# Transposing the probabilities of eleven pairs of heads in the DMA engines instead of TensorE

## Chip, cores and metric

One core of a Trainium2 chip. The metric is the device time of one execution in microseconds; below it is called the time. TensorE (PE, with its weight loads as PEld), VectorE (DVE), ScalarE (ACT) and GpSimd (POOL) compute, SyncE (SP) issues the DMA transfers.

## What is computed

Attention of 8 batches of 8 heads over 576 positions of 64 values, with a mask by blocks of 64 positions, then a mixer on the result: a step along the positions of rank 32, and a feed-forward step over 512 channels with 2048 hidden ones.

```
scores = scale * matmul(q, k.T);  masked where the key's block is later than the query's
attn = exp(scores - max);  attn = attn / (sum(attn) + 1e-09)
x = matmul(attn, v), heads side by side: [batch, 576, 512]
u = x + (x.T @ U @ V).T
out = u + max(u @ w_ch1, 0) @ w_ch2
```

## The kernel before

**Pairs of heads.** The 64 heads go in 32 pairs p of two heads s. The queries of a head lie in five blocks i: 64 queries in block 0, 128 in the others, and block i sees 128 i + 64 keys. `scores` multiplies queries by keys on TensorE in fp32, takes the largest score on VectorE (L1287) and the exponentials with their sums on ScalarE (L1298); they land in SBUF in `pt_r`, queries on the partitions. `normalise` inverts the sums (L1311, L1312) and scales the exponentials in place on GpSimd (L1319), twelve instructions to a pair. `transpose` turns them block by block on TensorE into PSUM (L1373), 26 to a pair, and eight copies to a pair bring them to `pw_r` in SBUF: on ScalarE (L1346), two of the eight on VectorE (L1344) from pair VP on. `apply_v` multiplies by V in fp32 (L1394): the two heads write the upper and lower 64 partitions of one bank, 16 instructions to each head. `mix` does the step along the positions (L1426 to L1480) and stores u.

**The mixer.** `ffn_chunk` does 768 of the hidden channels for chunks of 288 positions, two chunks to a batch, in three half-precision products for each fp32 one (L729, L754): 72 products in either line for each chunk. A chunk needs u of its batch, so its four pairs. `block_products` does the other 1280 channels for whole batches in seven products in place of eight (L978). It starts once all pairs are through (`end`), and has its weights split into high and low parts: `weights` casts them on ScalarE (L835) and subtracts on GpSimd (L831). The first weights go where the pool `ep` was, so they wait for what used that pool (`scored`, L811).

**The order of the work.** `Plan` takes each piece of work with an engine, an estimated duration, a rank and what it reads and writes. `issue` then plays the estimates through: an engine that is free takes the ready piece of the lowest rank. The sequence that comes out is the program of each engine, and at run time each engine follows its program in order and waits where something isn't ready. Pairs have ranks of 2000 p and some, mixer products on TensorE 1e6 and more, so these fill in where no piece of a pair is ready. Where nothing is ready in the first 130 us, a product of zeros is put in (L1560). `port` marks VectorE's pieces during which the plan starts none on GpSimd. VARIANT seeds a variation of +-2% on the estimates.

## Time and profile before

| | us |
|---|---|
| time, median of 3 runs (lowest, highest) | 1076.58 (1076.16, 1077.4) |
| time of the profiled execution | 1076.24 |
| its span, first to last instruction | 1074.4 |
| TensorE busy in the span | 1065.3 |
| VectorE, ScalarE, GpSimd busy | 850.3, 650.7, 346.3 |
[...]
| first and last product with V (L1394) | 24.6, 576.37 |
| DMA | 107.37 MB, 100 GB/s |

Busy time is the union of an engine's instructions. Products on TensorE overlap, so what one costs is read from one start to the next in the timeline, not from its duration. An engine's lines also say what ended the idle time before them.

### The profile page before, as it was taken

The numbers are of one execution on the slowest core, as the hardware profiler recorded it, in microseconds if no ns is written. First come the engines' busy times: TensorE is split into PE (matmuls) and PEld (weight loads), VectorE is DVE, ScalarE is ACT, GpSimd is POOL, SyncE is SP. The second block draws the span as 40 slices with busy tenths as digits, with TensorE's granted clock in tenths as the row PEclk, the third lists the DMA queues.
The fourth block names the chain that finished last, engine by engine and source line by source line (L and its number), as shares of the span: only waits on it lengthen the run. The fifth ranks groups of instructions, "written<-read, shape, count | busy, mean of one in ns | idle before, by whom it ended". The sixth has DMA issues, their size and how long they took to land.

```text
span 1074.4 us, 25473 instructions
## 1 busy us (share of the span) xinstructions
PE 1065.3 (99%) x9676; PEld 845.8 (79%) x9676; DVE 850.3 (79%) x1799; ACT 650.7 (61%) x1674; POOL 346.3 (32%) x624
## 2 busy tenths in 40 slices
PE   9999999999999999999999999999999999999998
PEld 7678867888787888888877777777777777777776
DVE  5879987887764665778856643999898989999998
ACT  6888777766766667577585542545454545454553
POOL 4744436556545455365376460000000000000000
PEclk9999999999999999999999999999999999999999
DMA  4453635453433241444222422040404031313111
GB/s 146 136 175 121 201 107 186 137 174 116 130 103 101 82 131 63 151 132 160 89 80 74 127 59 75 1 126 9 133 13 122 18 116 32 103 37 98 41 50 45
DMA packets 68266, 107.37 MB, mean 100 GB/s; under 512 B 6896, under 2 KB 50928, under 8 KB 68144
## 3 DMA queue, kind: packets, MB, share of 16 engines
q1 hardware_dynamic: 68144, 105.75, 31.8%
q8 instruction: 76, 1.25, 0.5%
q14 instruction: 46, 0.38, 0.1%
HBM read 76.23 MB, written 29.49 MB: 98 GB/s over the span
## 4 chain that ended last, share of the span: by engine, by line
PE 93%; ACT 3%; DVE 2%; POOL 1%; issue 1%; DMA 0%; ACTq 0%; POOLq 0%; DVEq 0%
PE bb L978 38%; PE bf L754 13%; PE bf L729 12%; PE ba L1373 8%; PE ba L1394 8%; PE bw L1262 5%; PE bq L1262 3%; ACT p L1298 2%; PE ba L1426 2%; PE ba L1452 1%; PE ba L1480 1%; PE bf L1560 1%; POOL p L1319 1%; POOL w1l L831 0%; PE bf L1120 0%
## 5 line engine op out<-in xcount | busy, mean ns | idle before, releaser
L1319 POOL TENSOR_SCALAR p<-p,rv 64x64 f32<-64x64 f32 (+4 forms) x384 | 183.5, 490 | 111.1 <-DVE rv L1312 35.3
L978 PE MATMUL bb<-ph,w2h 128*128 128x288 f16 x560 | 151.1, 286 | 0.0
L978 PE MATMUL bb<-ph,w2l 128*128 128x288 f16 x560 | 151.1, 286 | 0.0
L978 PE MATMUL bb<-ph,w1l 128*128 128x288 f16 x560 | 148.8, 286 | 0.0
L978 PE MATMUL bb<-ph,w1h 128*128 128x288 f16 x560 | 148.8, 286 | 0.0
L900 ACT CAST ph<-hb 128x576 f16<-128x576 f32 x144 | 84.3, 589 | 83.1 <-PE bb L978 82.0
L978 PEld LDWEIGHTS <-w1h 128*128 128x128 f16 x1120 | 109.3, 98 | 28.0
L978 PEld LDWEIGHTS <-w2h 128*128 128x128 f16 x1120 | 109.3, 98 | 27.9
L978 PE MATMUL bb<-pl,w2h 128*128 128x288 f16 x560 | 123.7, 286 | 0.0
L1287 DVE TENSOR_REDUCE mx<-bw 128x1 f32<-128x576 f32 (+2 forms) x192 | 76.2, 436 | 50.1 <-PE bw L1262 49.2
L978 PE MATMUL bb<-pl,w1h 128*128 128x288 f16 x560 | 114.5, 286 | 0.0
L754 PE MATMUL bf<-hh,w2h 128*128 128x288 f16 x384 | 110.3, 287 | 0.4 <-DVE hl L737 0.4
L754 PE MATMUL bf<-hh,w2l 128*128 128x288 f16 x384 | 110.0, 286 | 0.6 <-DVE w2l L543 0.6
L754 PE MATMUL bf<-hl,w2h 128*128 128x288 f16 x384 | 109.9, 286 | 0.0
L1373 PE MATMUL ba<-ident,p 128*128 128x128 f32 x668 | 102.2, 276 | 0.0
L1298 ACT ACTIVATE p<-bw,mx 128x192 f32<-128x192 f32 (+2 forms) x192 | 92.5, 489 | 13.9 <-DVE mx L1287 12.0
L1262 PE MATMUL bw<-raw 64*64 64x288 f32 (+4 forms) x896 | 97.0, 346 | 0.4 <-ACT p L1298 0.3
L902 DVE TENSOR_TENSOR pl<-hb,ph 128x576 f16<-128x576 f32 x144 | 91.2, 650 | 1.5
L729 PEld LDWEIGHTS <-w1h 128*128 128x128 f16 x768 | 74.2, 98 | 19.9 <-issue 2.3
L1262 PE MATMUL bq<-raw 64*64 64x384 f32 (+1 forms) x496 | 89.7, 470 | 0.1
L754 PEld LDWEIGHTS <-w2h 128*128 128x128 f16 x768 | 75.1, 98 | 18.5 <-ACT w2h L539 0.2
L1373 PEld LDWEIGHTS ba<-ident,p 128*128 128x128 f32 x668 | 76.8, 141 | 5.6 <-issue 1.6
(193 smaller groups left out, 2386.5 us busy)
## 6 DMA issues: line engine op xcount, KB each, us to landing
raw<-in_qk_dram SPq DMA_DIRECT2D x31, 576.0 KB, 3.9
o_d<-ot SPq DMA_DIRECT2D x72, 144.0 KB, 1.8
vr<-in_v_dram SPq DMA_DIRECT2D x32, 320.0 KB, 3.0
ur<-u_d SPq DMA_DIRECT2D x64, 144.0 KB, 2.3
wr<-o_d SPq DMA_DIRECT2D x32, 288.0 KB, 3.1
out_dram<-wr SPq DMA_DIRECT2D x31, 288.0 KB, 2.3
st<-in_w_dram SPq DMA_DIRECT2D x16, 512.0 KB, 4.2
u_d<-ut SPq DMA_DIRECT2D x28, 288.0 KB, 2.1
```

The lines of the kernel that those rows point to most:

```text
L729: nc.tensor.matmul(ps[:, :T], w()[wn][:, k, fs], m[k].ap, start=(i == 0), stop=(i == len(ops) - 1))
L754: nc.tensor.matmul(ps[:, :T], w()[wn][:, f, ms], hs[f][x].ap, start=(i == 0), stop=(i == len(ops) - 1))
L900: add("ACT", _act(n * T, True), E, lambda: nc.scalar.copy(h.ap[:, :n, :], x[0]()), [x[1]], [h])
L902: "DVE", _dve(n * T), E, lambda: nc.vector.tensor_sub(l.ap[:, :n, :], x[0](), h.ap[:, :n, :]), [x[1], h], [l],
L978: nc.tensor.matmul(bank[:, i, :T], x()[:, w(k)], p.ap[:, k, :], start=first and n == 0, stop=last and n == len(ops) - 1)
L1262: nc.tensor.matmul(o, raw[r, 64 * n : 64 * n + 64], raw[r, S + k0 : S + k1], start=True, stop=True)
L1287: lambda i=i, n=n: nc.vector.tensor_reduce(out=mx[: P if i else 64, n : n + 1], in_=view(i), op=ALU.max, axis=AX.XY if i == 4 else AX.X, n ...
L1298: return nc.scalar.activation(out.rearrange("p (j k) -> p j k", j=2) if i == 4 else out, view(i), AF.Exp, bias=mx[:rows, n : n + 1], accum ...
L1319: lambda: nc.gpsimd.tensor_scalar(out=out, in0=x, scalar1=iv, scalar2=1.0, op0=ALU.mult, op1=ALU.mult),
L1373: nc.tensor.transpose(out=to, in_=pt_r[i][h % PB[i]][:, j * P : (j + 1) * P], identity=perm.ap)
L1394: nc.tensor.matmul(bank[g][64 * s : 64 * s + 64, x : n[g]], vr[:, 5 * s + j, :], pw[g][s][:, _at(g, j)], start=(j == 0), stop=(j == NK[g] ...
L1426: nc.tensor.transpose(out=ps[:, i, :], in_=xt[:, j * P : j * P + rows], identity=ident.ap)
```

## The change

For the eleven pairs in XP (10, 12, ..., 30) `halve` takes the place of `normalise` and `transpose`, and `apply_x` that of `apply_v`. `halve` writes the scaled probabilities as two half-precision parts, a high part and what it leaves, side by side into `hl_of`: one buffer for the blocks 4, 1, 0 (8 blocks of 128 keys) and one for 3, 2 (7 blocks), both used by either half s of a pair. When a buffer is full, one transfer on SP's queue (`dma_start_transpose`) turns both parts into `turn_r`: two transfers for each s, four to a pair. Blocks 4, 1, 0 are scaled and cast on ScalarE and the low part is made on VectorE; blocks 3 and 2 are scaled on GpSimd, cast on ScalarE and subtracted on GpSimd. `apply_x` splits V into two such parts with a scale from its largest value, and multiplies in three half-precision products for each block of 128 queries by 128 keys, 90 to a pair, again with the two heads in the two halves of a bank; the copy out of PSUM takes the scale back.

The new buffers lie in the pool `ep`; `usf`, `xs` and `vf`, which the first four pairs use, now lie inside `turn_r`. The first block weights (`scored`) now also wait for all that uses the new buffers. Two memsets are added at the start, and VARIANT, NF (pairs that may use either group of banks), VP and MX (ranks of `mix`) have other values.

```diff
--- before.py
+++ after.py
@@ -58,24 +58,27 @@
 TAIL = {"PE": 165, "DVE": 78, "ACT": 105, "POOL": 20, "SP": 0}
 INTO = {"PE": 355, "DVE": 60, "ACT": 60, "POOL": 200, "SP": 60}
 NEAR, DL, PORT = 130, 3000, 200
-VARIANT = 176
+VARIANT = 229
 PEQ = 1450.0
 PVX = 150.0
-NF = 4
+NF = 6
 NS = 2
 BF = 1
 SL = 2500
 LATE = 150
 FROM = 180e3
 SL2 = 1985
-MX = (-500, -3000)
+MX = (-2000, -3000)
 WARM = 130e3
 IDLE = 56.0
-VP = 6
+VP = 10
 VEC = ((1, 1),)
 KP = 1
 START = {"PE": 4400, "DVE": 3100, "ACT": 2400, "POOL": 2700, "SP": 700}
 SPL = 5
+XP = tuple(range(10, 31, 2))
+XS, XC, XD = 1100.0, 0.65, 3500
+XG = (2, 3)
 FM = 4
 COL = 0.4555
 LA, MP = 900.0, 500.0
@@ -808,7 +811,7 @@
         def at(x, *i):
             return lambda: first()[x][(slice(None), *i)]
 
-        scored = after(*raw_r, xs, *usf.parts, *vf.parts)
+        scored = after(*raw_r, xs, *usf.parts, *vf.parts, *hl_of, vh, vl, *vs_r, *vi_r, *(b for r in turn_r for b in r))
 
         def weights(slots, by, sc, whole, room, split):
 
@@ -1154,9 +1157,16 @@
     ut_r = [b.split(2) for b in ring(ap, 1, [P, S], F32, "ut")]
     ust = buf(ap, [P, 5, 2 * R], F32R, "ust").split(2)
     v3 = buf(ap, [3 * R, S], F32R, "v3").split(2)
-    usf = buf(ep, [P, 5, R], F32, "usf").split(2)
-    vf = buf(ep, [R, S], F32, "vf").split(2)
-    xs = buf(ep, [P, 5, P], F32, "xs")
+    turn_r = [[buf(ep, [P, 2 * n, P], F16, f"turn{x}{g}") for g, n in enumerate((8, 7))] for x in range(2)]
+    place = f32(turn_r[0][0].ap.rearrange("p a b -> p (a b)"))
+    usf = Buf(place[:, : 5 * R].rearrange("p (j r) -> p j r", j=5)).split(2)
+    xs = Buf(place[:, 5 * R : 5 * R + 5 * P].rearrange("p (j d) -> p j d", j=5))
+    vf = Buf(f32(turn_r[1][0].ap.rearrange("p a b -> p (a b)"))[:R, :S]).split(2)
+    hl_of = [buf(ep, [P, 2, n * P], F16, f"hl16_{g}") for g, n in enumerate((8, 7))]
+    slot_of = {4: (0, 0), 1: (0, 5), 0: (0, 7), 3: (1, 0), 2: (1, 4)}
+    vh, vl = (buf(ep, [P, 10, D], F16, x) for x in ("vh", "vl"))
+    vs_r, vi_r = ring(ep, 2, [P, 2], F32, "vs"), ring(ep, 2, [P, 1], F32, "vi")
+    mv_r = [b.split(1) for b in ring(ep, 2, [P, 1], F32, "mv")]
 
 
     for j in range(4):
@@ -1165,6 +1175,9 @@
     for i, r in enumerate(pt_r[1:], 1):
         for p in r:
             nc.vector.memset(p[:, P * i + 64 :], 0.0)
+
+    for b in hl_of:
+        nc.vector.memset(b.ap, 0.0)
 
     def mixing_weights(prio):
 
@@ -1338,6 +1351,99 @@
                     corner(0, h)
         if s:
             corner(1, 2 * p)
+
+    def halve(p, s, pr):
+        slot = (2 * p + s) % 4
+        ss, rv = ss_r[slot], rv_r[slot]
+
+        def inverse():
+
+            nc.vector.tensor_reduce(out=rv.ap, in_=ss.ap, op=ALU.add, axis=AX.X)
+            nc.vector.reciprocal(rv.ap, rv.ap)
+            return nc.vector.tensor_scalar(out=rv.ap, in0=rv.ap, scalar1=2.0 ** 15, scalar2=1.0, op0=ALU.mult, op1=ALU.mult)
+
+        add("DVE", 340, pr, inverse, ss.parts, rv.parts)
+        for n, (x, i) in enumerate(job(p)):
+            side = (s, 1 - s)[x]
+            g, at = slot_of[i]
+            h, w, rows, both = 2 * p + side, P * i + 64, P if i else 64, hl_of[g]
+            pt, iv = pt_r[i][h % PB[i]], rv[:rows, n : n + 1]
+            hi, lo, x = both[:rows, 0, at * P : at * P + w], both[:rows, 1, at * P : at * P + w], pt[:rows, :w]
+            if i in XG:
+                add(
+                    "POOL", 255 + 0.85 * w, pr,
+                    lambda x=x, iv=iv: nc.gpsimd.tensor_scalar(out=x, in0=x, scalar1=iv, scalar2=1.0, op0=ALU.mult, op1=ALU.mult),
+                    [rv.parts[n]], [pt],
+                )
+                add("ACT", _act(w, True), pr, lambda hi=hi, x=x: nc.scalar.copy(hi, x), [pt], [both])
+                add("POOL", 60 + 2.2 * w, pr, lambda hi=hi, lo=lo, x=x: nc.gpsimd.tensor_sub(lo, x, hi), [pt, both], [both])
+            else:
+                add(
+                    "ACT", _act(w, True) + 105, pr, lambda hi=hi, x=x, iv=iv: nc.scalar.activation(hi, x, AF.Copy, scale=iv),
+                    [rv.parts[n], pt], [both],
+                )
+                add(
+                    "DVE", 60 + 1.3 * w, pr,
+                    lambda hi=hi, lo=lo, x=x, iv=iv: nc.vector.scalar_tensor_tensor(
+                        out=lo, in0=x, scalar=iv, in1=hi, op0=ALU.mult, op1=ALU.subtract
+                    ),
+                    [rv.parts[n], pt, both], [both], port=True,
+                )
+            if i in (0, 2):
+                to = turn_r[side][g]
+                add(
+                    "SP", XS + XC * 2 * P * (8, 7)[g], pr,
+                    lambda to=to, both=both: nc.sync.dma_start_transpose(out=to.ap, in_=both.ap.rearrange("p a k -> p (a k)")),
+                    [both], [to], after=XD,
+                )
+
+    def apply_x(p, pr):
+        xt, vr = xt_r[p % 2], vr_r[p % 2]
+        sc, iv, mu = take(vs_r, "vs"), take(vi_r, "vi"), take(mv_r, "mv")
+        largest(lambda: vr.ap.rearrange("p a b -> p (a b)"), 10 * D, vr, mu, 0, pr)
+        power(mu, 1, 2.0 ** 6, sc, pr, banks_p(p))
+        add(
+            "DVE", 70, pr,
+            lambda: nc.vector.tensor_scalar(out=iv.ap, in0=sc[:, 1:2], scalar1=2.0 ** -28, scalar2=1.0, op0=ALU.mult, op1=ALU.mult),
+            [sc], [iv], port=True,
+        )
+        add(
+            "POOL", 145 + 0.85 * 10 * D, pr,
+            lambda: nc.gpsimd.tensor_scalar(out=vr.ap, in0=vr.ap, scalar1=sc[:, 0:1], scalar2=1.0, op0=ALU.mult, op1=ALU.mult), [sc], [vr],
+        )
+        add("ACT", _act(10 * D, True), pr, lambda: nc.scalar.copy(vh.ap, vr.ap), [vr], [vh])
+        add("POOL", 60 + 2.2 * 10 * D, pr, lambda: nc.gpsimd.tensor_sub(vl.ap, vr.ap, vh.ap), [vr, vh], [vl])
+        bank = [Buf(pool=banks_p(p)) for _ in range(2)]
+        n = [QS[g + 1] - QS[g] for g in range(2)]
+        whole = [vh, vl, *(b for r in turn_r for b in r)]
+        order = Buf()
+
+        def products(g):
+            for i in ((0, 1, 2), (3, 4))[g]:
+                t, at = slot_of[i]
+                ops = [(j, v, a) for j in range(i + 1) for v, a in ((vh, 0), (vl, 0), (vh, 1))]
+                for m, (j, v, a) in enumerate(ops):
+                    w = P if j < i else 64
+                    x = max(P * i + 64 - QS[g] - w, 0)
+                    o = 64 if i and w == 64 else 0
+                    for s in range(2):
+                        nc.tensor.matmul(
+                            bank[g][64 * s : 64 * s + 64, x : x + w], v[:, 5 * s + j, :],
+                            turn_r[s][t][:, (8, 7)[t] * a + at + j, o : o + w], start=m == 0, stop=m == len(ops) - 1,
+                        )
+
+        for g in (1, 0):
+            cost = 3 * sum(2 * i + 4 + 0.425 * (P * i + 64) for i in ((0, 1, 2), (3, 4))[g])
+            add(
+                "PE", cost + PVX * g, pr if g else -1e5, lambda g=g: products(g), [*whole, *([] if g else [order])],
+                [bank[g], *([order] if g else [])], hold=xt.parts,
+            )
+        for g in (1, 0):
+            add(
+                "ACT", _act(n[g]) + 105, pr,
+                lambda g=g: nc.scalar.activation(xt[:, QS[g] : QS[g + 1]], bank[g][:, : n[g]], AF.Copy, scale=iv.ap),
+                [bank[g], iv], [xt.parts[g]],
+            )
 
     def copy(vector, n, pr, out, inp, reads, writes):
         if vector:
@@ -1529,12 +1635,19 @@
             load_qk(p + 1, max(pr - LA, 1.0))
         for s in range(2):
             scores(p, s, pr + 10 + 20 * s - (SL if p < NPAIR else SL2))
-            normalise(p, s, pr + 30)
-        for g in (1, 0):
-            for h in (2 * p, 2 * p + 1):
-                for part in range(2):
-                    transpose(h, g, part, pr + 40 + 10 * (1 - g))
-        apply_v(p, pr + 60)
+            (halve if p in XP else normalise)(p, s, pr + 30)
+        if p in XP:
+            if p == XP[0]:
+                for b in (turn_r[0][0], turn_r[1][0]):
+                    for x in (xs, *usf.parts, *vf.parts):
+                        b.readers += x.readers + x.writers
+            apply_x(p, pr + 40)
+        else:
+            for g in (1, 0):
+                for h in (2 * p, 2 * p + 1):
+                    for part in range(2):
+                        transpose(h, g, part, pr + 40 + 10 * (1 - g))
+            apply_v(p, pr + 60)
         if p + 1 < NH // 2:
             load_v(p + 1, pr + 1000)
         mix(p, pr + (MX[1] if p % NPAIR == NPAIR - 1 else MX[0]))
```

## Rows read from the trace of the kernel before

**Rows 1.** The page: busy time of each engine; shares of the chain that ended last, by line.
```profile
PE 1065.3 (99%) x9676; PEld 845.8 (79%) x9676; DVE 850.3 (79%) x1799; ACT 650.7 (61%) x1674; POOL 346.3 (32%) x624
...
PE bb L978 38%; PE bf L754 13%; PE bf L729 12%; PE ba L1373 8%; PE ba L1394 8%; PE bw L1262 5%; PE bq L1262 3%; ACT p L1298 2%; PE ba L1426 2%; PE ba L1452 1%; PE ba L1480 1%; PE bf L1560 1%; POOL p L1319 1%; POOL w1l L831 0%; PE bf L1120 0%
```

**Rows 2.** Busy us of each engine in two stretches, granted clock, DMA share, GB/s.
```profile
0.00:194.00 194.00, 189.09 (x1858) 143.50 (x1860) 158.47 (x451) 151.32 (x464) 98.22 (x200) 1.00 0.49 151
194.00:579.00 385.00, 384.39 (x3809) 310.39 (x3802) 274.96 (x675) 264.37 (x805) 206.62 (x386) 1.00 0.36 114
```

**Rows 3.** L729, L754, L978 alone after 579 us (PE, PEld); one piece of the chain.
```profile
579.00:1074.00 495.00, 36.71 (x288) 28.04 (x288) 1.00 0.23 69
...
579.00:1074.00 495.00, 44.19 (x348) 33.66 (x348) 1.00 0.23 69
...
579.00:1074.00 495.00, 412.58 (x3360) 328.08 (x3360) 1.00 0.23 69
...
637.55 8.82 PE bf L754 x72
```

**Rows 4.** From 194 to 560 us: all engines as in rows 2; L1373 alone; L1394 alone.
```profile
194.00:560.00 366.00, 365.64 (x3636) 295.55 (x3627) 262.54 (x660) 252.12 (x781) 195.30 (x380) 1.00 0.37 119
...
194.00:560.00 366.00, 79.55 (x520) 59.74 (x520) 1.00 0.37 119
...
194.00:560.00 366.00, 59.16 (x641) 40.93 (x641) 1.00 0.37 119
```

**Rows 5.** Timeline of TensorE: start us, us of the group, line, out<-in, form, count.
```profile
301.87 0.27 PE L1373 MATMUL ba<-swap,p 128*128 128x128 f32 x1
301.98 0.49 PE L1373 MATMUL ba<-ident,p 128*128 128x128 f32 x3
302.31 0.29 PE L754 MATMUL bf<-hh,w2h 128*128 128x288 f16 x1
...
303.35 0.41 PE L1452 MATMUL ba<-xl,ust 128*64 128x128 f32 x4
303.59 0.29 PE L1373 MATMUL ba<-swap,p 128*128 128x128 f32 x1
...
305.28 2.94 PE L1394 MATMUL ba<-spare,vr 128*64 128x256 f32 x32
308.15 0.40 PE L1480 MATMUL ba<-v,t 96*128 96x288 f32 x1
```

**Rows 6.** Instruction groups (busy us, mean ns): nearest shapes for copies, casts, subtractions, scalings.
```profile
L1346 ACT COPY pw<-ba 128x64 f32<-128x64 f32 (+1 forms) x113 | 50.8, 461 | 20.4 <-PE ba L1373 16.7 <-DVE mx L1287 1.7 <-DVE pw L1344 0.5
...
L1344 DVE COPY pw<-ba 128x512 f32<-128x512 f32 x32 | 21.8, 685 | 5.5 <-PE ba L1373 4.9 <-ACT tb L1459 0.3
...
L900 ACT CAST ph<-hb 128x576 f16<-128x576 f32 x96 | 63.7, 670 | 60.8 <-PE bb L978 59.8 <-DVE pl L902 1.0
...
L543 DVE SCALAR_TENSOR_TENSOR w1l<-wr,sc,w1h 128x384 f16<-128x384 f32 x8 | 5.5, 708 | 1.4 <-ACT w1h L539 1.4
...
L713 POOL TENSOR_TENSOR ul<-us,uh 128x288 f16<-128x288 f32 x56 | 40.1, 731 | 28.0 <-ACT uh L712 13.2 <-DVE spare L831 3.3 <-ACT ph L907 3.0
...
L1319 POOL TENSOR_SCALAR p<-p,rv 64x64 f32<-64x64 f32 (+4 forms) x384 | 183.5, 490 | 111.1 <-DVE rv L1312 35.3 <-DVE z L423 12.4 <-DVE wr L431 11.9
```

**Rows 7.** DMA issues: out<-in, queue, count, KB each, median us to landing.
```profile
st<-in_w_dram SPq DMA_DIRECT2D x16, 512.0 KB, 4.2
...
st<-in_U_dram SPq DMA_DIRECT2D x1, 128.0 KB, 5.9
```

**Rows 8.** VectorE's first reduction with the wait before it; the filler products of L1560.
```profile
9.19 1.14 DVE L1287 TENSOR_REDUCE mx<-bw 128x1 f32<-128x576 f32 x3 [6.13 <-PE bw L1262]
...
L1560 PE MATMUL bf<-zero 128*128 128x128 bf16 x192 | 13.5, 224 | 0.6 <-DVE ur L1487 0.6
```

**Rows 9.** L831 on GpSimd (shortest, median, longest ns, first and last start); chain's last piece.
```profile
L831 POOL TENSOR_TENSOR w1l<-wr,w1h x7: 2615/2622/2627, 551.9 to 585.1; 128x1280 f16<-128x1280 f32 x7
...
664.01 407.20 PE bb L978 x3324
```

## What is predicted

> **What bounds the kernel now.** I read the page first (busy shares, then the shares of the chain that ended last), then busy time by stage, then which products are left after the last pair, and last the timeline of single products. TensorE is busy 99% of the span and no other engine over 79%; the chain is made of TensorE lines almost alone [rows 1]. From 194 us to the last pair's product (579 us) TensorE works 384.4 of 385 us, VectorE 71%, ScalarE 69%, GpSimd 54%; before 194 us TensorE lacks 4.9 us [rows 2]. So time is TensorE's list of work. Two kinds of work share the middle stage: pairs of heads, which the planner ranks first, and the products of the mixer's chunks (L729, L754), which fill what the pairs leave. At 579 us 288 and 348 of these fill products are still to come, beside 3360 block products, and 72 of them take 8.82 us of the chain [rows 3]. A chunk has 144 of them (72 each in L729 and L754), and only the last batch's two chunks have to wait for the last pair; so 636 - 288 = 348 products at 0.122 us, 43 us, are a stock that could have run earlier. That stock decides what a slower pair costs: nothing, until it is used up.
>
> **What leaves TensorE.** Between 194 and 560 us 641 products of L1394 ran, 32 to a pair, so 20 pairs at 18.3 us each; with 520 transposes, 26 to a pair [rows 4]. In the timeline four transposes stand between two mixer products from 301.87 to 302.31: 0.11 us each, 2.86 us a pair. The product with V goes from 305.28 to 308.15: 2.87 us [rows 5]. Together 5.73 us a pair. (The chain gives L1373 and L1394 8% each, 86 us over 32 pairs, 2.7 us: the same.)
>
> **What comes to TensorE.** Per pair 90 half-precision products: for each of 15 blocks three (high by high, low by high, high by low), for two heads. 60 have 128 columns, 30 have 64, and each has its own load of 64 weights. No row shows this form. The nearest is L1452, 64 weights and 128 columns in one pass: four of them from 303.35 to 303.59, 0.06 us each with the load [rows 5]. The second question is whether the two heads, which write the two halves of one bank, share that time. In the old product each head has 1600 columns, two instructions for each; at the 0.85 ns a column of the transposes (0.11 us for 128) one head alone would take 2.7 us, and both took 2.87 [rows 5]. So heads do share, and I count 45 steps. With 0.06 us for each the sum is 2.7 us; if the 15 narrow steps cost half, 2.25; if nothing is shared, 90 x 0.06 = 5.4. I take 2.6, near the first, because a narrow step still loads the same weights, and add one transpose of 0.11 for the scale of V. Saved: 5.73 - 2.71 = 3.0 us a pair, **33 us** in eleven pairs (2.92 to 3.37 us, so 32 to 37, while heads share; 0.2 us a pair, 2.4 us, if they don't).
>
> The old product shows full 128-row weights of one head going in beside the other head's product [rows 5]. [...]
>
> **What comes to the other engines.** Per pair, by the rows of the nearest shape [rows 6]:
> ScalarE loses six copies of 0.46 us and gets ten casts (0.67 us at 576 columns, about 0.25 at 64: 4.6 us for both heads) and one of V (0.7): +2.6 us.
> VectorE loses two copies of 0.69 and gets six subtractions with a scale (0.71 us at 384 columns; 576, 192 and 64 wide about 3.0 us), the largest of V (0.7) and the small steps of its scale (about 1.1): +3.5 us.
> GpSimd loses twelve scalings of 0.49 and gets four, four subtractions (0.73 us at 288 columns; 3.8 us at 320 and 448), and a scaling and a subtraction on V (2.2): +2.3 us.
> In eleven pairs that is 29, 38 and 25 us. VectorE then needs 275 + 38 = 313 us in this stage. TensorE's work up to the last pair, with the stock moved ahead, is 579 - 33 + 43 = 589 us, so 395 us from 194 on, and VectorE keeps up if it works 79% of the time. It worked 82% in the first 194 us [rows 2]. So I put these at nothing, hidden beside the fill products; without that cover they are the second rival.
>
> **The transfers.** Four per pair, 0.52 or 0.46 MB each, all on SP's queue. They add 21.6 MB to the middle stage, 59 GB/s beside the 119 there, whose share was 0.37 [rows 4]. The planner counts 1.1 + 0.65 ns x 2048 = 2.4 us on SP and 3.5 to landing. No row shows a transfer that transposes. A plain load of 512 KB lands in 4.2 us; the load of U, 128 KB in runs of 256 bytes, took 5.9, which four times over is 23.6 [rows 7]. I take 6 us, near the plain load: the source has runs of 3.6 and 4 KB, as that load has. The product now waits for them; behind it on TensorE's list stand fill products and the next scores. On SP a transfer that waits for its halves holds up the loads and stores queued behind it. At 6 us the wait is in the place the order gives it, and costs nothing; at the ends it is the slower rival.
>
> No run here shows the rate. [...]
>
> **Small things.** Two memsets on VectorE at the start (3840 halves) lie in the 6.1 us for which it waits before its first reduction [rows 8]. In pairs 6 to 9 eight copies go from VectorE to ScalarE; NF and MX shift banks and ranks, and the new VARIANT shuffles ties. These can't be read from rows; TensorE's lack before 194 us (4.9 us, and 13.5 us of filler products of L1560 [rows 8]) is the most they could win, and I take 0, with 4 us either way. The first block weights now wait for pair 30's product, not for the last scores: its low parts ran on GpSimd from 551.9 to 588 us, and the block products are alone on TensorE from 664 on [rows 9]. Pair 30's product stood one pair's time ahead of the last, at about 560, so this is 8 us later (551.9 to 560), while fill products last from 588 to 664: nothing, 8 us without that cover.
>
> **The sum.** The profiled run took 1076.24 us, span 1074.4, the median of three is 1076.58. 1076.2 - 33 = **1043 us**; with the bounds of the products (32 to 37) and 4 us for the small things, 1035 to 1049.
>
> **Rivals.**
> *The helpers set the pace* (0.17). TensorE stays full only while VectorE works 79% of the stage. Against: the first stage's 82%. For: before 579 it never had to pass 71% here, and its list is in order. At 75%, 313 / 0.75 = 418 us, the last pair ends at 612, TensorE stands 22 us: 1065. This case runs from 1049 to 1072.
> *Heads don't share* (0.07): 2.4 us saved, 1074.
> *The transfers land late* (0.10), the slower end. Both halves of a pair use one buffer per group of blocks (hl16), so the second half's parts wait until the first half's two transfers have read it. One such pair occupies it for 2 x (about 4 us of halving + 2 T), T being the time of one transfer if they don't overlap, and must fit in the time of two pairs, 36.6 us: T up to 7.2 us is free. Beyond that the last pair moves back by eleven times the excess. It can come at 589 us before TensorE stands; at 622, 43 us behind where it is now, standing has eaten the 33 us. 43 / 11 is a cycle of 40.5 us, so T = 8.1 us is the point from which it decides. At T = 8.5 the last pair ends at 638, TensorE stands 49 us, and the time is 1092. For: 23.6 us at the far bound. Against: the plain load's 4.2, and transfers of one queue that overlap.
> The rest: 0.63 for the forecast, 0.03 for under 1035.
>
> About 0.2% (2 us) is what a measurement of this kernel can tell from no change. Faster: the forecast, what lies below, nearly all of the helpers' case and half of the unshared heads, 0.85; same: 0.04; slower: 0.11. The range goes from 1034 to 1068: it leaves out the late transfers, the unshared heads and the tail of the helpers' case, 0.2.
>
> **What would show it.** Right: the new products step by about 0.06 us per two and take 2.3 to 2.8 us per pair; TensorE stays over 98% from 194 us to the last pair; that pair's product comes between 545 and 590 us, with fewer than 636 fill products left if it is late; transfers land in 4 to 7 us. Wrong: idle TensorE before the new products, released by a DMA; VectorE over 85% with TensorE under 97%; a product over 4.5 us.

## The result

The changed kernel takes 1050.06 us (median of four runs, 1049.68 to 1050.55), the kernel before 1076.65 beside it: a ratio of 0.9753, 95% interval 0.9736 to 0.977. That is 26.6 us less; 33 were forecast, and 1043 us. The range, 1034 to 1068, holds it. Some line numbers moved: the transposes of TensorE are now L1479, the old product with V L1500, the chunks' products L732 and L757, the block products L981, and the new products L1430.

The page after, as rows 1 gave it for before: busy time of each engine, DMA packets, the chain by engine and its costliest lines.

```profile
span 1048.8 us, 26253 instructions
...
PE 1029.6 (98%) x9978; PEld 816.3 (78%) x9978; DVE 880.0 (84%) x1947; ACT 680.8 (65%) x1737; POOL 375.0 (36%) x602
...
DMA packets 154159, 129.06 MB, mean 123 GB/s; under 512 B 92784, under 2 KB 136816, under 8 KB 154032
...
PE 87%; DVE 5%; ACT 5%; DMA 1%; issue 1%; POOL 1%; SPq 0%; POOLq 0%; ACTq 0%
PE bb L981 39%; PE bf L757 12%; PE bf L732 10%; PE bw L1275 5%; PE ba L1500 5%; PE ba L1479 4%; PE bq L1275 3%; ACT p L1311 2%; PE ba L1430 2%; DVE mx L1300 1%; PE ba L1532 1%; PE ba L1558 1%; DMA vr<-in_v_dram 1%; PE ba L1586 1%; DVE hl L740 1%
```

The chain by engine before:

```profile
PE 93%; ACT 3%; DVE 2%; POOL 1%; issue 1%; DMA 0%; ACTq 0%; POOLq 0%; DVEq 0%
```

TensorE still bounds the kernel. Its transposes and old products went from 8% each of the chain [rows 1] to 4% and 5%; what took their place is 2%. But VectorE and ScalarE are now 10% of the chain, 5% before: in more places than before TensorE waits for them. These waits are short, as TensorE stands still for 19.2 us of the span in all (1048.8 - 1029.6), 9.1 before.

Windows of the trace after: start:end, length, busy us of TensorE, its weight loads, VectorE, ScalarE and GpSimd with their instructions, granted clock, DMA share, GB/s. The first answers to rows 4; the others are what is left after 570 us, all engines, then L732 and L757 alone (TensorE, loads), as in rows 3.

```profile
194.00:560.00 366.00, 361.24 (x4224) 291.36 (x4225) 302.64 (x820) 281.03 (x848) 226.32 (x373) 1.00 0.75 181
570.00:1048.00 478.00, 473.92 (x3874) 378.47 (x3874) 418.92 (x669) 235.34 (x398) 43.52 (x33) 1.00 0.24 69
...
570.00:1048.00 478.00, 28.28 (x216) 20.97 (x216) 1.00 0.24 69
...
570.00:1048.00 478.00, 34.62 (x270) 26.26 (x270) 1.00 0.24 69
```

The last pair's product ends at 569.8 us. It came only 9 us earlier than before (567.0 against 576.37), though its stage had 33 us and more less to do: 486 fill products stand behind it in place of 636 [rows 3], so 150 products of 0.122 us, 18 us of the stock, were moved ahead into it. That is the trade the prediction counted on; 198 of the 348 spare ones were not needed.

The timeline of TensorE after, around one group of the new products (start, us, line, out<-in, form, count), and the same group in the chain:

```profile
307.50 0.28 PE L1430 MATMUL ba<-turn,vh 128*64 128x128 f16 x4
307.61 0.22 PE L1430 MATMUL ba<-turn,vl 128*64 128x128 f16 x2
...
308.68 0.20 PE L1430 MATMUL ba<-turn,vl 128*64 128x64 f16 x2
308.71 0.23 PE L1430 MATMUL ba<-turn,vh 128*64 128x64 f16 x4
...
307.43 2.27 PE ba L1430 x90
```

Two products of 128 columns, one for each head, step by 0.055 us (307.50 to 307.61 is two such steps). Two of 64 columns step by 0.03 (308.68 to 308.71). The last line gives 2.27 us for a pair: narrow steps do cost half, which was the lower bound, 2.25; 2.6 had been taken.

### The profile page after: what moved, and what is told of

It reads as the page before. It is cut to its first block, busy times and chain, and to the rows that moved or that the text cites. A ratio compares the mean times of both kernels' runs of the same rounds, so it can differ in the third digit from the quotient of the medians.

```text
span 1048.8 us, 26253 instructions
## 1 busy us (share of the span) xinstructions
PE 1029.6 (98%) x9978; PEld 816.3 (78%) x9978; DVE 880.0 (84%) x1947; ACT 680.8 (65%) x1737; POOL 375.0 (36%) x602
## 4 chain that ended last, share of the span: by engine, by line
PE 87%; DVE 5%; ACT 5%; DMA 1%; issue 1%; POOL 1%; SPq 0%; POOLq 0%; ACTq 0%
PE bb L981 39%; PE bf L757 12%; PE bf L732 10%; PE bw L1275 5%; PE ba L1500 5%; PE ba L1479 4%; PE bq L1275 3%; ACT p L1311 2%; PE ba L1430 2%; DVE mx L1300 1%; PE ba L1532 1%; PE ba L1558 1%; DMA vr<-in_v_dram 1%; PE ba L1586 1%; DVE hl L740 1%
## 5 line engine op out<-in xcount | busy, mean ns | idle before, releaser
L981 PE MATMUL bb<-ph,w2h 128*128 128x288 f16 x560 | 151.0, 286 | 0.0
L981 PE MATMUL bb<-ph,w2l 128*128 128x288 f16 x560 | 151.0, 286 | 0.0
L981 PE MATMUL bb<-ph,w1l 128*128 128x288 f16 x560 | 148.7, 286 | 0.0
L981 PE MATMUL bb<-ph,w1h 128*128 128x288 f16 x560 | 148.7, 286 | 0.0
L1332 POOL TENSOR_SCALAR p<-p,rv 128x576 f32<-128x576 f32 (+3 forms) x252 | 121.0, 492 | 53.3 <-DVE rv L1325 11.9
L981 PEld LDWEIGHTS <-w1h 128*128 128x128 f16 x1120 | 109.6, 98 | 27.7
L981 PEld LDWEIGHTS <-w2h 128*128 128x128 f16 x1120 | 109.6, 98 | 27.7
L981 PE MATMUL bb<-pl,w2h 128*128 128x288 f16 x560 | 123.5, 286 | 0.0
L757 PE MATMUL bf<-hh,w2h 128*128 128x288 f16 x384 | 110.4, 287 | 4.7 <-DVE ot L769 2.6
L981 PE MATMUL bb<-pl,w1h 128*128 128x288 f16 x560 | 114.3, 286 | 0.0
L757 PE MATMUL bf<-hl,w2h 128*128 128x288 f16 x384 | 110.1, 287 | 0.0
L757 PE MATMUL bf<-hh,w2l 128*128 128x288 f16 x384 | 110.1, 287 | 0.0
L1311 ACT ACTIVATE p<-bw,mx 128x192 f32<-128x192 f32 (+2 forms) x192 | 92.5, 489 | 24.5 <-DVE mx L1300 23.4
L732 PEld LDWEIGHTS <-w1h 128*128 128x128 f16 x768 | 74.1, 98 | 22.1 <-issue 4.4
L757 PEld LDWEIGHTS <-w2h 128*128 128x128 f16 x768 | 75.7, 99 | 19.2 <-issue 0.7
L1275 PEld LDWEIGHTS bw<-raw 64*64 64x64 f32 x896 | 65.4, 134 | 19.2 <-issue 5.9
L1311 ACT ACTIVATE p<-bq,mx 128x448 f32<-128x448 f32 x124 | 71.1, 578 | 0.1
```

The lines of the kernel that those rows point to most:

```text
L732: nc.tensor.matmul(ps[:, :T], w()[wn][:, k, fs], m[k].ap, start=(i == 0), stop=(i == len(ops) - 1))
L757: nc.tensor.matmul(ps[:, :T], w()[wn][:, f, ms], hs[f][x].ap, start=(i == 0), stop=(i == len(ops) - 1))
L981: nc.tensor.matmul(bank[:, i, :T], x()[:, w(k)], p.ap[:, k, :], start=first and n == 0, stop=last and n == len(ops) - 1)
L1275: nc.tensor.matmul(o, raw[r, 64 * n : 64 * n + 64], raw[r, S + k0 : S + k1], start=True, stop=True)
L1311: return nc.scalar.activation(out.rearrange("p (j k) -> p j k", j=2) if i == 4 else out, view(i), AF.Exp, bias=mx[:rows, n : n + 1], accum ...
L1332: lambda: nc.gpsimd.tensor_scalar(out=out, in0=x, scalar1=iv, scalar2=1.0, op0=ALU.mult, op1=ALU.mult),
```

## Where the gain went

For this the kernel before isn't the best neighbour, since VARIANT, NF, VP and MX changed too. The first run takes all pairs out of XP and keeps those values (and the two memsets and the places of the buffers).

```diff
-XP = tuple(range(10, 31, 2))
+XP = ()
```

> XP is empty: no pair is turned by the DMA engines, all else (seed 229, NF 6, VP 10, MX, the added memsets) is as in the changed kernel. The changed kernel's new products take 2.28 us a pair, so by starts on TensorE about 37 us were saved, and 26.6 came out; the 10 us between show as TensorE idle and at half clock mostly from 85 to 210 us, where only the first of the eleven pairs begins. Theory A: the new planner values are worth little (0 with 4 us either way, as in the prediction): 1073 to 1081 us. Theory B: they cost the early 10 us: 1083 to 1089 us. Theory C: they are where the gain comes from: under 1070.

It took 1078.63 us, ratio 1.0019 (1.001 to 1.0029): what was kept costs 2.2 us, and the eleven pairs are worth 28.6. The second run does the reverse, pairs with the old values.

```diff
-VARIANT = 229
+VARIANT = 176
-NF = 6
+NF = 4
-MX = (-2000, -3000)
+MX = (-500, -3000)
-VP = 10
+VP = 6
```

> The eleven pairs as in the changed kernel, but seed 176, NF 4, VP 6 and MX (-500, -3000) of the kernel before. Theory A: 1046 to 1054 us. Theory B, the values cost the early 10 us: about 1040. Theory C, the values carry a part of the gain: 1058 or more.

1050.85 us, 0.9757 (0.9741 to 0.9774): with the pairs in, the values make no difference that shows. So the pairs are the whole gain, and the four values give none of it.

A ledger of TensorE: the time from each start to the next one, summed by line over the whole trace of either kernel (waits after an instruction are in it).

| | no pairs | eleven pairs | difference |
|---|---|---|---|
| transposes, L1479 | 100.7 (832) | 67.5 (546) | -33.2 |
| old product with V, L1500 | 92.3 (1024) | 60.5 (672) | -31.8 |
| new products, L1430 | 0 | 25.1 (990) | +25.1 |
| scale of V and the like, L487 | 3.1 | 4.5 | +1.5 |
| fill products, L732 and L757 | 284.9 | 293.7 | +8.8 |
| block products, L981 | 411.5 | 411.5 | 0 |
| all other lines | | | +0.8 |

The edit itself gives 38.4 us; the rows sum to -28.8, and -28.6 was measured. The 9.6 us that are missing are nearly all at fill products, whose number is unchanged (1152 in either line): most of it is time in which TensorE stood or ran at half clock. Two such places stand out. The timeline of TensorE after, and then of the kernel without pairs, at 160 us (in brackets the idle time and who ended it):

```profile
159.70 0.27 PE L1532 MATMUL ba<-ident,xt 128*64 128x128 f32 x1
162.39 0.65 PE L732 MATMUL bf<-uh,w1h 128*128 128x288 f16 x4 [2.41 <-DVE hl L740]
```
```profile
159.66 0.27 PE L1532 MATMUL ba<-ident,xt 128*64 128x128 f32 x1
162.34 0.65 PE L732 MATMUL bf<-uh,w1h 128*128 128x288 f16 x4 [2.41 <-DVE hl L740]
```

This wait is the same without a single pair, and the run with the pairs and the old values hasn't got it (no wait over 1.1 us before 600 us): it came with the other values. The chain of the changed kernel shows what is late. The subtraction L740 on VectorE wants ScalarE's cast L737, and that stands on ScalarE's list behind four pieces of 0.8 us that scale the two parts of a weight of the mixer (L588):

```profile
158.24 1.66 ACT w2h L588 x2
159.90 1.65 ACT w2l L588 x2
161.55 0.30 ACT hh L737
...
161.87 0.47 DVE hl L740
...
162.39 0.90 PE bf L732 x6
```

The second wait belongs to the pairs: without them TensorE stands for 0.35 us at this place (204 us). SyncE's queue after, and the chain there:

```profile
191.83 6.01 SPq L1396 DMA_TRANSPOSE turn<-hl  x2
197.95 1.01 SPq L1609 DMA_DIRECT2D u_d<-ut  x1
199.01 0.93 SPq L608 DMA_DIRECT2D st<-in_w_dram  x2
...
198.09 0.59 DVE pw L1450
198.68 0.29 SPq L1609
199.01 5.16 DMA st<-in_w_dram
204.19 0.50 ACT z L442
...
207.38 0.33 PE ba L1479
```

Two transfers of the first turned pair hold the queue until 197.84 us: from 191.83, when the first one's buffer has just been written (191.80), for 4.35 us, then for 1.56. Behind them stands a store of u, which by the chain waits for VectorE until 198.68, and behind that the load of a weight. ScalarE's list waits for that weight (L442), and TensorE stands for 1.89 us until the copies behind it have freed a bank. So the chain names the store and not the transfers; that these have a part is shown by the run with eight transfers (below): there four hold the queue from 191.21 to 199.29, the load goes out at 199.96, and TensorE stands for 2.63 us. How the 1.89 us divide between transfers and store is not shown. TensorE's time by stretches, after, then without pairs, then for the run with the pairs from 14 on (below):

```profile
150.00:200.00 50.00, 46.20 (x441) 36.03 (x433) 40.12 (x117) 39.66 (x114) 26.05 (x47) 0.97 0.65 157
200.00:250.00 50.00, 47.77 (x583) 37.44 (x581) 40.59 (x108) 37.42 (x115) 28.59 (x47) 0.97 0.71 183
```
```profile
150.00:200.00 50.00, 46.62 (x454) 36.68 (x448) 40.34 (x106) 37.52 (x110) 25.54 (x52) 0.97 0.44 135
200.00:250.00 50.00, 49.65 (x485) 40.17 (x483) 43.25 (x110) 34.08 (x111) 28.07 (x57) 1.00 0.49 151
```
```profile
150.00:200.00 50.00, 48.30 (x484) 37.98 (x481) 39.13 (x107) 37.47 (x112) 26.38 (x54) 1.00 0.49 145
200.00:250.00 50.00, 50.00 (x491) 40.79 (x490) 40.03 (x104) 36.21 (x112) 27.53 (x53) 1.00 0.51 149
```

Behind each of the two waits the granted clock is at a lower level, 0.5 of the full one, for 3.4 us, at 163.8 and 208.2 us: that is the 0.97. Each of these two waits therefore costs its own time and some 1.7 us more. From 150 to 250 us the pairs so cost 2.3 us of TensorE's time (93.97 busy against 96.27) and one more stretch at half clock, 1.7. In all, TensorE's gaps of over 0.1 us add up to 13.3 us in the changed kernel, 8.3 without pairs and 4.0 before; 3.5 us of the 13.3 lie behind 210 us (1.0 at 364, 0.8 at 590, 0.7 at 509), 0.3 of the 8.3. So 4 of the missing 9.6 us are in that stretch and 3.2 are later waits. Of the other 2.4 some 1.6 lie in the change from fill products to other work. Between fill products the step is 0.12 us; from the last of them to a new product it is 0.23, nine times, and to a score 0.22, eight times more than without pairs. Where the rest lies is open.

So the pairs 10 and 12, the first two, meet the stage in which the mixer's weights are still loaded and split. The next run leaves these two as they were: nine pairs, from 14.

```diff
-XP = tuple(range(10, 31, 2))
+XP = tuple(range(14, 31, 2))
```

> XP is 14, 16, ..., 30: pairs 10 and 12, which fall into the stage where the helpers also split weights, are turned by TensorE as before: nine pairs. Theory A, the 8 us are lost in that stage alone: nine pairs give 9 x 3.4 = 30 us from 1078.6, so 1047 to 1050. Theory B, the loss is spread over all pairs, 0.8 us each: 1078.6 - 9 x 2.6 = 1055.

1049.79 us, 0.9754 (0.9739 to 0.9768). Nine pairs are worth 28.8 us, 3.2 each, as much as the eleven. At that price the first two would save 6.4 us, and the changed kernel loses as much in the stretch above (46.20 + 47.77 us busy against 48.30 + 50.00, and two stretches at half clock against none). Not all of that is theirs: the wait at 160 us, which the kernel without pairs has in full, is shorter here too.

Does the piece L588 make the wait at 160 us? With nine pairs that gap is 1.48 us. Here its rank is raised, so that the plan puts it after the pairs' pieces.

```diff
-                    "ACT", _act((e - k) * CW, True) + 100, -1.0,
+                    "ACT", _act((e - k) * CW, True) + 100, 2.2e4,
```

> The nine pairs from 14 on, and ScalarE's scaling of the second half of w2 (L588, 3.3 us in one piece at 158 us, rank -1, ahead of everything) gets rank 22000, between pairs 10 and 12, so that the casts on which the fill products wait go first. Theory A, TensorE's 1.5 us of idle time at 159 us come from it: 1046 to 1049. Theory B, only the sequence changes and that moves the time by some 3 us either way, as seed 230 did: 1047 to 1054.

1048.76 us, 0.9742 (0.9725 to 0.9758); the largest gap there is now 0.58 us, at 164, and the gaps sum to 9.8 us in place of 10.5. One wait less, but others come in its place (1.55 us at 467, 1.13 at 322): 1 us at most. And another seed, all else as in the changed kernel:

```diff
-VARIANT = 229
+VARIANT = 230
```

> The changed kernel with the planner's seed at 230 in place of 229, nothing else. How far does the sequence alone move the time? Theory A (the values are worth little, 4 us either way): 1046 to 1056. Theory C (this seed carries a part of the gain): 1058 or more.

1053.1 us, 0.9775 (0.9759 to 0.9791), with 19.2 us of gaps. The sequence that the plan happens to find is worth 3 us by itself. Shown is that with this seed the first two pairs add nothing, that the wait at 160 us is the sequence's and not the pairs', and that a sequence can be 3 us worse or so. Not shown is that the first two pairs would add nothing in every sequence: eleven and nine pairs were compared in one sequence each. A sequence without these waits was not found, and the times of the eleven, the nine and the nine with the later piece lie within 1.3 us of each other.

## Do the heads share TensorE?

The loop over the two heads is put outside: each head's products run by themselves.

```diff
-                for m, (j, v, a) in enumerate(ops):
-                    ...
-                    for s in range(2):
+                for s in range(2):
+                    for m, (j, v, a) in enumerate(ops):
+                        ...
```

> The same 90 products of a new pair, but all of one head's for a block of queries before the other's, so that neighbours no longer write different halves of the bank; nothing else changes. Theory A, two heads share a step: alone a product costs 0.05 to 0.06 us (128 columns) or 0.03 to 0.06 (64), 4.2 to 5.4 us a pair in place of 2.28, so 21 to 34 us more: 1071 to 1084. Theory B, the weight load sets the step and sharing gives nothing: 1050.

1061.49 us, 0.9856 (0.9841 to 0.9871): 11.4 us more. The timeline of TensorE in that kernel and a group in its chain:

```profile
309.26 0.28 PE L1430 MATMUL ba<-turn,vh 128*64 128x128 f16 x2
309.37 0.22 PE L1430 MATMUL ba<-turn,vl 128*64 128x128 f16 x1
309.43 0.25 PE L1430 MATMUL ba<-turn,vh 128*64 128x128 f16 x3
...
309.02 3.50 PE ba L1430 x82
```

A single product of 128 columns now steps by the 0.055 us that two took before (309.26 to 309.37 is two). So the heads did share: 3.50 us against 2.27, 1.23 a pair, 13.5 in eleven, close to the 11.4 measured. The time lies between the two theories. Single narrow products step by 0.03 us (five of them from 309.51 to 309.68), which gives 60 x 0.055 + 30 x 0.03 = 4.2 us, the low end of theory A; the rest down to 3.50 is that heads still overlap where one head's run meets the other's. So this run prices only a part of the rival of unshared heads: with 4.2 us a pair it is an estimated 21 us slower than the changed kernel, 1071, near the 1074 of the prediction.

## Are the transfers and the helpers hidden?

The transfers after: duration on SyncE's queue (ns, shortest, median, longest) and landing.

```profile
L1396 SPq DMA_TRANSPOSE turn<-hl x44: 1322/2138/4354, 176.1 to 551.6; - x44
...
DMA to landing us min/median/max: 4.0/4.7/7.2
```

Three runs take the suspects away or make them worse. The first keeps only the first pair's four transfers, which are those of the queue at 191.8 us above; the later pairs multiply what these left, and 40 transfers are missing from the time.

```diff
-    lambda to=to, both=both: nc.sync.dma_start_transpose(...)
+    lambda to=to, both=both: p == XP[0] and nc.sync.dma_start_transpose(...)
```

> Only pair 10 issues its four transfers; the other ten new pairs multiply what lies in the buffers (left out: 40 of 44 transfers). Order and all other work stay as they are. Theory A: the transfers are in time and hidden, as no TensorE idle time in the changed kernel was ended by one: 1047 to 1050 us. Theory B: their lateness, or what they hold up on SP and in the DMA engines, is where the missing 10 us went: 1040 to 1044.

1048.76 us, 0.974 (0.9726 to 0.9755). Its window from 194 to 560 us, to be held against the first window of the changed kernel:

```profile
194.00:560.00 366.00, 361.49 (x4269) 293.34 (x4268) 301.14 (x818) 283.19 (x850) 225.01 (x372) 1.00 0.41 127
```

The DMA engines' share falls from 0.75 to 0.41, TensorE's busy time stays. Without the 40 transfers the median is 1.3 us lower, no more than runs of one kernel differ. The first pair's four are still in it, and so is the wait behind them, 1.81 us here. The second run sends each part by itself, 88 transfers of half the size:

```diff
-    lambda ...: nc.sync.dma_start_transpose(out=to.ap, in_=both.ap.rearrange("p a k -> p (a k)"))
+    lambda ...: [nc.sync.dma_start_transpose(out=to[:, n * a : n * a + n, :], in_=both[:, a, :]) for a in range(2)]
```

> The high and the low part of a buffer are turned by a transfer each, eight to a pair in place of four, in the same place of SP's list. Theory A: the transfers have slack, since leaving out 40 of 44 gave 1.3 us; SP takes 1.3 to 4.4 us for one, so four more hold its queue some 4 to 8 us longer per pair: 1049 to 1054 us. Theory B: the products wait as soon as transfers come later (a place in TensorE's list that was set for four): 1060 or more, with TensorE idle time ended by DMA turn.

1048.83 us, 0.9736 (0.9721 to 0.9752). Packing the parts side by side saves nothing in time: the halves land in 3.4 us each, and there was slack for twice the issues. The third run makes the low parts of the probabilities in their first column only; the rest of them is not computed.

```diff
-    nc.gpsimd.tensor_sub(lo, x, hi)
+    nc.gpsimd.tensor_sub(lo[:, :1], x[:, :1], hi[:, :1])
-    out=lo, in0=x, scalar=iv, in1=hi, op0=ALU.mult, op1=ALU.subtract
+    out=lo[:, :1], in0=x[:, :1], scalar=iv, in1=hi[:, :1], op0=ALU.mult, op1=ALU.subtract
```

> The subtractions that make the low parts of the probabilities, on VectorE and GpSimd, work on one column each (left out: nearly all of the low parts); order and all else stay. That takes about 2 us from VectorE and 3 us from GpSimd in each of eleven pairs. By starts on TensorE the new pairs save 37 us, the new planner values cost 2 (1078.6 without pairs), and some 8 us go to idle TensorE and waits that only come with the pairs. Theory A: these 8 us are the added work on the helpers in their ordered lists: 1041 to 1046 us. Theory B: they come from something else (the first pair's place in the order, the weight load behind the transfers at 199 us): 1048 to 1051.

1048.65 us, 0.974 (0.9722 to 0.9759). The same window:

```profile
194.00:560.00 366.00, 361.68 (x4255) 292.52 (x4254) 283.27 (x818) 281.00 (x848) 193.33 (x370) 1.00 0.74 181
```

VectorE has 19 us less to do and GpSimd 33, and TensorE gets 0.4 us of it in this stage. The helpers' durations are hidden. The three times differ from the changed kernel's by 1.2 to 1.4 us each, with runs of one kernel up to 5 us apart; what they show is that the 40 later transfers, their number and the subtractions do not hold the missing 9.6 us. The first pair's transfers are in all three runs.

## From which point the transfers decide

The slower rival named a mechanism, the one set of buffers hl16, and a price for it. Alternate pairs give it two pairs' time; neighbours do not. Two runs ask for that.

```diff
-XP = tuple(range(10, 31, 2))
+XP = (14, 15, 17, 18, 20, 21, 23, 24, 26, 27, 29, 30)
```

> Twelve pairs, two of three from 14 on (14, 15, 17, 18, ..., 30), so that neighbours share the one set of buffers hl16 and turn. Theory A, a pair behind the early stage is worth its 3.4 us of TensorE whatever its neighbour is: 1078.6 - 12 x 3.4 = 1038. Theory C, the cycle of the one set of buffers decides, as in the late-transfer rival: with 4.7 us to landing and some 2 us on SP a new pair occupies it for 2 x (4 + 2 + 4.7) = 21 us, while a pair has 17 us, so neighbours move the last pair back by some 5 us for each couple, 30 us in all, past the 24 us of fill products that the changed kernel still has at 570 us: 1044 to 1055.

1072.71 us, 0.9962 (0.9949 to 0.9975): twelve pairs, and nearly nothing gained. From pair 14's products (268.1 us) to pair 29's (557.7) three pairs take 57.9 us, so each 19.3 although two of them are cheaper for TensorE than the 18.3 of before. From a turned pair to its turned neighbour it is 28 us in the mean (24.5 to 32.2), from a turned pair over an old one to the next turned one 29 (24.5 to 32.9): a step of the turned pairs takes about the same, whether or not an old pair stands between.

```diff
-XP = tuple(range(10, 31, 2))
+XP = tuple(range(14, 31))
```

> All seventeen pairs from 14 to 30. Theory A (each worth 3.4 us): 1021. Theory C (the cycle of 21 us or more against 16 to 17 us for a pair): the last pair moves back by 17 x 4 to 5 us, 70 to 85; the 24 us of stock and what TensorE saved are used up and it stands: 1060 to 1090. VectorE would need 275 + 17 x 2.7 = 321 us from 194 us on and is no longer the first bound if the stage is that long.

1153.32 us, 1.0711 (1.0695 to 1.0727), slower than expected by any theory. A window of it, its products L1430 with first and last start, the group of pair 25 in the chain, who waits for the transfers L1396, and TensorE's longest waits:

```profile
194.00:560.00 366.00, 310.69 (x3601) 247.18 (x3594) 281.94 (x767) 249.63 (x721) 194.59 (x286) 0.91 0.76 178
...
L1430 PE MATMUL ba<-turn,vh x1020: 192/219/317, 264.1 to 667.1; 128*64 128x128 f16 x135, 128*64 128x64 f16 x35
...
543.83 2.27 PE ba L1430 x90
...
  ACT hl L1382: 13.7, 6
  PE ba L1430: 11.1, 8
  ACT hl L1378: 8.5, 9
...
PE ba L1586 <- ACT t L1569: 24.1, 7, 7.9
PE bw L1275 <- ACT p L1311: 19.0, 11, 5.3
```

TensorE works 310.69 of 366 us at 0.91 of the clock; VectorE only 77%. A pair takes (667.1 - 2.3 - 264.1) / 16 = 25.0 us; up to pair 25 it is (543.8 - 264.1) / 11 = 25.4, and 24.2 from there on. ScalarE waits for transfers before it may write hl again (L1382, L1378), and what stands behind these casts on its list, the exponentials and copies, makes TensorE wait. This reads like the one set of buffers, but helpers with too much to do could look alike. The last run tells them apart. The second half s of a pair gets a set of hl of its own (in room that the spare probabilities had) for pairs 14 to 25; 26 to 30 keep the one set for both.

```diff
+    both_r = spare[:, : 15 * P].bitcast(F16)
+    hl2_of = [Buf(both_r[:, a * P : b * P].rearrange("p (a k) -> p a k", a=2)) for a, b in ((0, 16), (16, 30))]
...
-    ..., hl_of[g]
+    ..., (hl2_of if s and p < PS else hl_of)[g]
```

> The same seventeen neighbouring pairs turned by the DMA engines as in the run of all pairs from 14, but with a second set of the buffers hl for one of the two halves of the keys in pairs 14 to 25 (it lies where the spare probabilities lay); pairs 26 to 30 keep the one set. Theory C (the cycle of the one set, written by VectorE, ScalarE and GpSimd, turned over SP, landed, multiplied, sets the 23.1 us from one product group to the next): pairs 15 to 25 step by 16 to 19 us, where the single turned tile comes next (four transfers of 2.1 us on SP, 4.7 us to land, 2.3 us of product), and pairs 26 to 30 stay near 23 us. Theory H (the helpers' own work sets the step): about 23 us in both stretches. The whole time then lies between 1050 and 1153 us by C, at 1150 by H; the step of the product groups is what tells the two apart.

(The 23.1 us in that text is too low, it is 25.0; and the half with the second set is the second half s of a pair, not of the keys.) The products, L1432 here, up to the group of pair 25 and from it on; two windows, of the first stretch and of the second:

```profile
L1432 PE MATMUL ba<-turn,vh x720: 192/219/316, 271.4 to 486.6; 128*64 128x128 f16 x120, 128*64 128x64 f16 x60
...
L1432 PE MATMUL ba<-turn,vh x360: 192/219/316, 484.5 to 612.5; 128*64 128x128 f16 x119, 128*64 128x64 f16 x61
...
290.00:530.00 240.00, 220.50 (x2802) 173.13 (x2796) 201.71 (x565) 183.13 (x540) 146.50 (x206) 0.99 0.95 214
530.00:650.00 120.00, 80.29 (x905) 62.39 (x906) 74.45 (x171) 69.76 (x160) 68.17 (x76) 0.80 0.60 133
```

With two sets a pair takes (484.5 - 271.4) / 11 = 19.4 us, with one set in the same kernel (612.5 - 2.3 - 484.5) / 5 = 25.1. The same pairs up to 25 took 25.4 with one set throughout. The helpers' work per pair is the same in all of these. So the cycle of the one set is the bound where pairs are neighbours, and with the second set for twelve of the seventeen pairs the time is 1099.24 us (one run): that takes back 54 of the 77 us by which the run with one set was slower than the kernel before. TensorE's clock goes along with it, 0.99 in the first stretch and 0.80 in the second, where TensorE often stands; how much of the 25.1 is the lower clock was not separated. The 19.4 is a little over the 16 to 19 expected, and something else is then near its end: the DMA engines are busy 95% of that stretch, more than any other row here shows. Whether they or the single turned tile set the 19.4 stays open, as does why the step is 28 to 29 us where two of three pairs are turned and not the 25 of the cycle.

## Why the prediction was right, and where it was off

- **What bounds the kernel** held: TensorE's list. From 194 to 560 us it worked 98.7% of the time (361.24 of 366). With nine pairs each brings 3.2 us; 3.0 were counted.
- **What leaves TensorE**: 5.73 us a pair were counted; the ledger gives 65 / 11 = 5.9, waits included.
- **What comes to it**: 2.6 was too much, 2.27 measured. "A narrow step still loads the same weights" was the reason that failed: narrow steps take 0.03 us with the load. The bound of 2.25 was the right one. The scale of V cost 0.14 (1.5 / 11), 0.11 was taken.
- **Heads share**: shown by the run with the heads apart, 3.50 us for a group in place of 2.27. In both traces the load of a new product covers all 128 rows and lasts 0.11 us (106 to 113 ns), while products of 128 columns, each with its own load, step by 0.055 us, of one head alone too. So loads overlap products here; what lets them is not shown.
- **The helpers**: +29, +38 and +25 us were summed for ScalarE, VectorE and GpSimd. Between 194 and 560 us they rose by 29, 40 and 31 [rows 4], but the helpers' share of the 150 fill products moved ahead is in that. Over the whole span, against the kernel without pairs, it is 30, 30 and 28 (680.8 - 650.7, 880.0 - 850.0, 375.0 - 347.1): VectorE's part was put too high, 2.7 us a pair in place of 3.5. VectorE at 83% (302.64 of 366) did keep up, so the bar of 79% was no obstacle.
- **The stock of fill products** took up what the pairs lost, 18 of its 43 us.
- **The transfers**: 6 us taken, 4.7 measured, hidden. Their rate was open: at the 159 GB/s of the last section 0.52 MB are an estimated 3.3 us in the DMA engines.
- **The slower rival** did not come about, since the cycle is 2 x (4 + 2 x 4.7) = 26.8 us by its formula with the landing time for T, and 25 to 29 measured, under the 36.6 us that alternate pairs have. Its mechanism holds, and its formula comes near: where pairs are neighbours they have 18.3, and the kernel is slower by 7%.
- **Small things** is the step that failed. They were put at 0, with 4 us either way, and where the first pairs fall wasn't looked at. Against the 38.4 us that the edit gives stand 2.2 for what the run without pairs keeps and the 9.6 of the ledger, 4 of these between 150 and 250 us, where pairs are turned while weights still come in on the same queue and are split on ScalarE. The first stage had shown TensorE's only lack, 4.9 us [rows 2]; the prediction read it as something to win, not as the sign that one more transfer on SP or one more cast on ScalarE has no cover there. That a transfer "holds up the loads and stores queued behind it" was said, and priced at nothing; at 198 us it was a store, and behind that a weight load. The two errors, 5.4 us too little saved (38.4 - 33) and 11.8 too little lost, make the 6.4 by which the saving fell short.
- **Luck**: the first of these errors hid almost half of the second. The sum's own bounds, 1035 to 1049 (1076.2 - 32 + 4 is 1048), were missed by 1 to 2 us; the range holds 1050 because it goes on to 1068 for the rival of the helpers, and in the run with narrow subtractions these did not set the pace.

## What to carry to other kernels

Here the saving on the bounding engine arrived in full only where that engine had other work ready; ask of the first instances of a change what they displace in the stage they fall into, since two of eleven added nothing here. A buffer written, transferred and written again has a cycle that is computed beforehand from the landing time, and compared with how often it is wanted: the same edit gave 2.5% at every other pair and cost 7% at every pair. A stock of independent products behind the bound decides what a slower side path costs, so count it first.

## What the runs showed of the hardware

- A transposing transfer of this size, SBUF to SBUF, takes the DMA engines about twice as long for a byte as the others here. From 194 to 560 us the 40 missing transfers are 54 GB/s (181 - 127) and 0.34 of the share (0.75 - 0.41): 159 GB/s for a full share, while the rest moves 127 / 0.41 = 310. They come in packets of some 250 bytes (86 thousand more under 512 B than before). Others land somewhat later beside them: the load of 576 KB in 4.6 us, the store of u in 3.6, where without the 40 it is 4.2 and 3.1 (4.2 and 3.2 without pairs).
- A transposing instruction holds SyncE's queue for 2.1 us in the median, 1.3 to 4.4; half-sized ones for 1.26. The wait for its source lies ahead of that: the one that took 4.35 us started at 191.83, and the last write of its buffer ended at 191.80.
- A half-precision product of 128 columns with its own load of 64 weights steps by 0.055 us, one of 64 columns by 0.03, and two that write the two halves of a bank share the step (2.27 us a pair, 3.50 with the heads apart).
- A wait of 1.9 us on TensorE was followed by 3.4 us at the lower clock in one kernel (208 us); in the run with 40 transfers left out a wait of 1.8 us in the same place was not. Half of 3.4 is 1.7, near the 1.3 us by which that run is faster; that the one makes the other is not shown. The length of one wait doesn't decide it: with the other seed a wait of 1.96 (492 us) was not followed by the lower clock (1.00 from 194 to 560 us, with the 3.4 at 197 in it), while 1.04 and 1.49 close together (190 and 193) were, for 3.4 us at 197 (0.97 from 150 to 200).
